# Linear attention with two MLPs: the maxima of k and q and the sums of q as rows through DRAM in blocks 2 to 8

## The chip, the cores and the metric

The kernel runs on one core of a Trainium2 chip. The metric is the device time in microseconds (us) of one execution; 1617.67 us is the median of three runs of the kernel before (1616.58, 1617.67, 1617.69). The profile was taken in an execution of its own. TensorE is called PE, VectorE DVE, ScalarE ACT, GpSimd POOL, and SyncE SP; SP issues nearly all the DMAs.

## The reference

```
q, k, v: 8 batches x 8 heads x 576 x 64, f32
q_s = exp(q - max over the 64);   q_s = q_s / (sum over the 64 + 1e-9)
k_s = exp(k - max over the 576);  k_s = k_s / (sum over the 576 + 1e-9)
kv  = k_s^T v   (64 x 64 for each batch and head);   attention = q_s kv
x = attention as 4608 tokens x 512
x = elu(x @ w_in) @ w_out                       (512 -> 2048 -> 512)
h = x @ w_in2;  P = a0 + a1 h + a2 h^2 + a3 h^3
Q = 1 + |b0| |h| + |b1| h^2;  out = (P / (Q + 1e-6)) @ w_out2
```

The weights w_out of both layers come as 64-bit floats, as does w_in; the kernel makes f32 of their bits itself.

## The kernel before

The 4608 tokens are cut into nine blocks of 512 (NB = 9, j = 0 to 8), the hidden 2048 into 16 parts of 128 (KF = 16, f). One tile (L, j, f) is one part of one block in one layer: `plan_in` multiplies the block's x (four pieces of 128 x 512) with a part of w_in into a PSUM bank (L726 to L728), an elementwise chain makes g of it (`plan_elu`, or `plan_rational` in layer 1), and `plan_out` adds g times a part of w_out into four accumulators (L768). Each f32 operand is split into a high and a low fp32r part (`copy_hi` L269, `sub_lo` L272) and each product is three matmuls, so a tile is 12 + 12 matmuls of 128 x 512. There are 2 x 9 x 16 = 288 tiles. Tiles 0 to 31 are blocks 0 and 1 of layer 0, taken in parts (CUT); block j from 2 on begins at tile 16 j, and layer 1 at tile 144.

In layer 0 the attention of the next block runs between the tiles. It goes by pairs of heads: pair n = 4 j + hp covers q of block j (512 tokens) and k and v of batch j (576 tokens) for two heads. Blocks 0 and 1 are done by `plan_pair`, blocks 2 to 8 by `plan_late`. Block 8 has no batch of its own, so k and v end with n = 31 and q with n = 35.

For q, tokens lie on the partitions: `q_max` (DVE), `q_sub` (POOL), `q_exp` (ACT), `q_sum` and `q_rec` (DVE), `q_mul` (POOL), then four transposes on PE (`q_T`, L504) and a copy out of PSUM (`q_copy`, ACT, L509), which gives qT with heads and features on the partitions. For k, `k_max` (L438, DVE) takes the maximum of the five tokens that lie on a partition, a transpose on PE (`k_maxT`, L442) and a small `k_top` (L446, DVE) finish it over the partitions, and a second transpose (`k_row`, L450) of the broadcast column gives the row in PSUM that `k_sub` (L453, DVE) subtracts; `k_exp` (ACT) follows, and `kv_mm` (L464, PE) multiplies with v, with a column of ones that gives the sum. `kv_norm` and `kv_div` make kvd. `plan_x` multiplies qT and kvd for two pairs (`x_mm`, L545) and splits the result into the x of layer 0.

`plan_unit(n)` puts into one PE operation: the four transposes of q for n, `k_maxT` of n + 2, `k_row` of n + 1, and `kv_mm` of n. The program is written out by `Plan`: a list scheduler in the program that holds a cost for each operation, starts at each turn the one that can start earliest (then by due time), and writes each engine's instructions in that order. What really waits is decided on the chip by the data and the buffers. A step number r is a tile: `in_ops[tiles[r]]` as a condition means that the plan lets the operation start only when that tile's input matmuls are done, and `at_step(n)` gives the step of pair n: 21, 23.5, 26, 28.5 for block 2, and 4 n - 17 from n = 12 on. The limits on buffers (`kind`) are two for kt, two for qt, one for x. SP issues its DMAs in the order of the plan, and each waits in the queue until its data or its buffer is there.

Of the kernel before, what the change touches and what calls it, by code (L numbers as in the profile page):

```python
# [30 lines left out]
class Plan:  # L31
# [81 lines left out]
    def run(self):  # L113
# [48 lines left out]
def linear_attention_elu_rational(  # L162
# [183 lines left out]
    def plan_w2(f, which, rank, after):  # L346

        b = {}

# [4 lines left out]

        def high():
            return b["st"][:, :, 1].bitcast(F32)

# [6 lines left out]
        b["op"] = op(SP, load, after, rank, take=["st"], dma=1.3)  # L364
# [37 lines left out]
    def pair_fns(n):  # L402
# [6 lines left out]
        kkind, vkind, qkind = (("kt", "x") if j > 1 else "kt", "vb", "qt") if not first else (  # L409
# [26 lines left out]
        def k_max(e):
            km = b["km"] = at.tile([P, 2 * D], F32, tag="km", name="km", bufs=2)
            nc.vector.tensor_reduce(out=km, in_=b["kt"].rearrange("p j n -> p n j"), op=ALU.max, axis=AX.X)  # L438

        def k_maxT(e, ps=None):  # L440
            b["mt"] = (bank() if ps is None else ps)[:, 0:P]
            nc.tensor.transpose(b["mt"], b["km"], ident)  # L442
# [64 lines left out]
        def q_copy(e):  # L507
# [3 lines left out]
        b.update({f.__name__: f for f in (load_k, load_v, load_q, k_max, k_maxT, k_top, k_row, k_sub, k_exp, kv_mm, kv_norm,  # L511
                                          kv_div, q_max, q_sub, q_exp, q_sum, q_rec, q_mul, q_T, q_copy)})
        return b

    def plan_q(n, r, gate, ahead):
# [3 lines left out]
        b["q_op"] = lq = chain("load_q", (SP, b["load_q"], [gate and in_ops[tiles[int(r) - 2]]], r - 3), take=[qkind], dma=0.66)  # L519
        o = chain("q_max", (DVE(0.67), b["q_max"], [lq, gate], r))  # L520
# [4 lines left out]
        return chain("q_mul", (either, b["q_mul"], [o], r + 1.2), extra=ahead)  # L525
# [38 lines left out]
    def plan_pair(j, hp, r):  # L564
# [4 lines left out]
        o = plan_q(n, r, None, 0.0)  # L569
# [46 lines left out]
    def at_step(n):  # L616
        return max(4.0 * n - 17, 2.5 * n + 1)

    def plan_k(n):

        b = pair_fns(n)
        r = at_step(n - 2)
        b["k_op"] = l = chain("load_k", (SP, b["load_k"], [in_ops[tiles[int(r) - 3]]], r - 3), take=[b["kinds"][0]], dma=0.83)
        b["km_op"] = chain("k_max", (DVE(1.3), b["k_max"], [l, in_ops[tiles[int(r) - 1]]], r - 1), take=["km"], extra=AHEAD)

    def plan_unit(n, q_ready=None):

        r = at_step(n)
        first_k, last_k = 2 * NP, B * NP
        has = [first_k <= m < last_k for m in (n + 2, n + 1, n)]  # L630
        b = [pair_fns(m) if ok else None for m, ok in zip((n + 2, n + 1, n), has)]
        mine = pair_fns(n)
        if has[2]:
            lv = chain("load_v", (SP, mine["load_v"], [in_ops[tiles[int(r) - 3]]], r - 2), take=["vb"], dma=0.83)

        def unit(e):
            if q_ready:
                mine["q_T"](e)
            ps = bank() if any(has) else None
            if has[0]:  # L640
                b[0]["k_maxT"](e, ps)
            if has[1]:
                b[1]["k_row"](e, ps)
            if has[2]:
                b[2]["kv_mm"](e, ps)

        need, free, take = [in_ops[tiles[int(r)]]], [], ["bank"] if any(has) else []
        if has[0]:
            need.append(b[0]["km_op"])
            free.append(("km", b[0]["km_op"]))  # L650
        if has[1]:
            need.append(b[1]["top_op"])
            free.append(("top", b[1]["top_op"]))
        if has[2]:
            need += [b[2]["exp_op"], lv]
            free += [(b[2]["kinds"][0], b[2]["k_op"]), ("vb", lv)]
            take.append("kvd")
        if q_ready:
            need.append(q_ready)
            free.append(("qt", mine["q_op"]))  # L660
            take += ["bank", "qT"]
        u = chain("unit", (PE(0.15 + 0.1 * has[0] + 0.1 * has[1] + 0.65 * has[2] + 0.4 * bool(q_ready)), unit, need, r + 1),
                  take=take, free=free, extra=0.2)
        done = []
        if has[0]:
            b[0]["top_op"] = o = chain("k_top", (DVE(0.3), b[0]["k_top"], [u], r + 1.1), take=["top"], extra=AHEAD)
            done.append(o)
        if q_ready:
            mine["t_op"] = u
            mine["qc"] = chain("q_copy", (ACT(), mine["q_copy"], [u], r + 1.1), extra=AHEAD)  # L670
        if has[1]:
            o = chain("k_sub", (DVE(0.85), b[1]["k_sub"], [u], r + 1.2))
            done.append(o)
            b[1]["exp_op"] = chain("k_exp", (ACT(0.75), b[1]["k_exp"], [o], r + 1.3), extra=AHEAD)
        if has[2]:
            o = chain("kv_norm", (DVE(0.33), mine["kv_norm"], [u], r + 1.15))
            kv_ready[n] = o = chain("kv_div", ((("ACT", 0.31), ("DVE", 0.25)), mine["kv_div"], [o], r + 1.2), extra=AHEAD)
            kvd_of[n] = u
            done.append(o)
        if done:  # L680
            at_ops.append(op((("", 0.0),), lambda e: None, done, r, free=[("bank", u)]))
        if q_ready:
            at_ops.append(op((("", 0.0),), lambda e: None, [mine["qc"]], r, free=[("bank", u)]))

    def plan_late(j, hp):
        n = j * NP + hp
        if n == 2 * NP:
            for m in (n, n + 1):
                plan_k(m)
                plan_unit(m - 2)  # L690
        if n + 2 < B * NP:
            plan_k(n + 2)
        r = at_step(n)
        plan_unit(n, plan_q(n, r - 1, in_ops[tiles[int(r) - 1]], AHEAD))
        if hp % 2:
            plan_x(n, r, [state[n - 1]["qc"], state[n]["qc"]])
# [355 lines left out]
def _laid_out(name, a, np):  # L1052
# [3 lines left out]
    if name == "q":  # L1056
        b, h, s, d = a.shape
        a = a.transpose(0, 2, 1, 3).reshape(b * s // TB, P, 4, h // 2, 2 * d).transpose(0, 3, 1, 2, 4)
        a = a.reshape(b * s // TB, h // 2, P, 4 * 2 * d)
# [42 lines left out]
```

## Time and profile before

| what | value |
|---|---|
| runs | 1616.58, 1617.67, 1617.69 us |
| profiled execution | 1616.44 us |
| its span in the profile | 1614.7 us |
| PE, ACT, DVE, POOL busy | 98%, 63%, 61%, 48% of the span |
| mean granted clock of PE | 0.995 |
| bytes moved by DMA | 114.82 MB, 71 GB/s over the span |

A row of the page names a line of the kernel, an engine, an operation, and out<-in by the program's names. Busy time is the union of a group's instructions; the duration of one matmul is longer than its distance to the next, because they are pipelined. A wait is idle time of an engine, put down to the instruction that ended it.

### The profile page before, as it was taken

The numbers are of one execution on the slowest core, as the hardware profiler recorded it, in microseconds if no ns is written. First come the engines' busy times: TensorE is split into PE (matmuls) and PEld (weight loads), VectorE is DVE, ScalarE is ACT, GpSimd is POOL, SyncE is SP. The second block draws the span as 40 slices with busy tenths as digits, with TensorE's granted clock in tenths as the row PEclk, the third lists the DMA queues.
The fourth block names the chain that finished last, engine by engine and source line by source line (L and its number), as shares of the span: only waits on it lengthen the run. The fifth ranks groups of instructions, "written<-read, shape, count | busy, mean of one in ns | idle before, by whom it ended". The sixth has DMA issues, their size and how long they took to land.

```text
span 1614.7 us, 21797 instructions
## 1 busy us (share of the span) xinstructions
PE 1584.6 (98%) x8040; PEld 1364.2 (84%) x8040; DVE 979.9 (61%) x1390; ACT 1018.6 (63%) x1688; POOL 772.0 (48%) x562
## 2 busy tenths in 40 slices
PE   6999999999999999999999999999999999999998
PEld 4788888888888888888888888888888888888886
DVE  7897655445344444321125777776868677777676
ACT  6766544454454544443557777777777777777675
POOL 3334333333233322333566666666566666666554
PEclk9999999999999999999999999999999999999999
DMA  8522533232233222110433010101000010100000
GB/s 322 203 118 89 166 120 103 100 114 86 102 102 115 85 92 81 61 40 14 124 93 103 8 53 1 52 1 39 15 26 28 20 34 10 43 8 21 1 27 26
DMA packets 48778, 114.82 MB, mean 71 GB/s; under 512 B 5664, under 2 KB 5664, under 8 KB 46624
## 3 DMA queue, kind: packets, MB, share of 16 engines
q1 hardware_dynamic: 48096, 112.10, 20.1%
q8 instruction: 63, 1.03, 0.3%
q10 hardware_dynamic: 576, 1.33, 0.2%
q14 instruction: 43, 0.35, 0.1%
HBM read 84.05 MB, written 29.36 MB: 70 GB/s over the span
## 4 chain that ended last, share of the span: by engine, by line
PE 87%; issue 4%; ACT 4%; DVE 2%; POOL 2%; DMA 1%; POOLq 0%; SPq 0%; DVEq 0%; ACTq 0%
PE acc L768 42%; PE ps L726 14%; PE ps L728 14%; PE ps L727 14%; POOL gs L272 2%; PE ps L464 1%; PE ps L545 1%; PE ps L504 1%; ACT p L871 1%; ACT s L867 1%; ACT m L877 0%; DMA hc<-w 0%; DMA kt<-in_k_dram 0%; ACT m L880 0%; PE acc L464 0%
## 5 line engine op out<-in xcount | busy, mean ns | idle before, releaser
L726 PE MATMUL ps<-xs,w_in 128*128 128x512 f32 x1152 | 438.8, 381 | 1.8 <-DVE p L892 1.7
L727 PE MATMUL ps<-xs,w_in 128*128 128x512 f32 x1152 | 436.6, 379 | 0.0
L728 PE MATMUL ps<-xs,w_in 128*128 128x512 f32 x1152 | 436.6, 379 | 0.0
L768 PE MATMUL acc<-gs,w_out 128*128 128x512 f32 x1728 | 407.1, 383 | 5.9 <-POOL gs L272 3.2
L272 POOL TENSOR_TENSOR gs<-m,gs 128x512 fp32r<-128x512 f32 x130 | 177.9, 1369 | 413.4 <-ACT gs L269 413.4
L768 PEld LDWEIGHTS acc<-gs,w_out 128*128 128x128 f32 x1728 | 324.9, 190 | 58.3 <-POOL gs L272 4.7
L838 DVE SCALAR_TENSOR_TENSOR m<-m,ps 128x512 f32<-128x512 f32 x144 | 98.9, 687 | 291.8 <-ACT m L835 278.9
L726 PEld LDWEIGHTS ps<-xs,w_in 128*128 128x128 f32 x1152 | 217.7, 189 | 37.2 <-issue 5.3
L728 PEld LDWEIGHTS ps<-xs,w_in 128*128 128x128 f32 x1152 | 217.7, 189 | 30.8
L727 PEld LDWEIGHTS ps<-xs,w_in 128*128 128x128 f32 x1152 | 217.7, 189 | 30.5
L874 POOL TENSOR_TENSOR s<-s,m 128x512 f32<-128x512 f32 x144 | 219.4, 1524 | 12.6 <-ACT m L863 12.6
L272 POOL TENSOR_TENSOR gs<-p,gs 128x512 fp32r<-128x512 f32 x72 | 116.1, 1613 | 211.7 <-issue 172.8
L768 PE MATMUL acc<-w_out,gs 128*128 128x512 f32 x864 | 200.9, 382 | 2.8 <-ACT gs L269 1.6
L768 PE MATMUL acc<-w_out,g 128*128 128x512 f32 x864 | 199.8, 379 | 0.5 <-POOL g L272 0.5
L832 ACT ACTIVATE m<-ps 128x512 f32<-128x512 f32 x144 | 85.8, 596 | 178.3 <-PE ps L728 122.5
L768 PEld LDWEIGHTS acc<-w_out,gs 128*128 128x128 f32 x864 | 164.3, 190 | 27.5 <-ACT gs L269 2.0
L768 PEld LDWEIGHTS acc<-w_out,g 128*128 128x128 f32 x864 | 163.2, 189 | 24.0 <-POOL g L272 0.9
L892 DVE SCALAR_TENSOR_TENSOR p<-p,a_sb,ps 128x512 f32<-128x512 f32 x144 | 107.5, 747 | 91.2 <-ACT m L863 91.1
L871 ACT ACTIVATE p<-ps,a_sb 128x512 f32<-128x512 f32 x144 | 112.2, 779 | 79.1 <-POOL gs L272 73.4
L269 ACT ACTIVATE gs<-m 128x512 fp32r<-128x512 f32 x144 | 90.4, 628 | 112.5 <-PE acc L768 97.7
L883 DVE SCALAR_TENSOR_TENSOR s<-s,m 128x512 f32<-128x512 f32 x144 | 135.4, 940 | 24.1 <-ACT m L880 23.9
L896 DVE SCALAR_TENSOR_TENSOR p<-p,a_sb,m 128x512 f32<-128x512 f32 x144 | 142.0, 986 | 2.3
(102 smaller groups left out, 1817.5 us busy)
## 6 DMA issues: line engine op xcount, KB each, us to landing
kt<-in_k_dram SPq DMA_DIRECT2D x32, 320.0 KB, 3.1
x<-e SPq DMA_DIRECT2D x36, 256.0 KB, 2.0
e<-x SPq DMA_DIRECT2D x36, 256.0 KB, 3.1
out_dram<-e SPq DMA_DIRECT2D x36, 256.0 KB, 2.0
vb<-in_v_dram SPq DMA_DIRECT2D x28, 325.0 KB, 3.4
bits<-in_moe_w_in_dram SPq DMA_DIRECT2D x8, 1024.0 KB, 10.3
qt<-in_q_dram SPq DMA_DIRECT2D x32, 256.0 KB, 3.2
bits<-in_moe_w_out_dram SPq DMA_DIRECT2D x8, 1024.0 KB, 11.9
```

The source lines that it names most:

```text
L269: nc.scalar.activation(out=hi, in_=src, func=AF.Copy)
L272: engine[e].tensor_tensor(out=lo, in0=src, in1=hi.bitcast(F32), op=ALU.subtract)
L726: nc.tensor.matmul(o, w[:, 0, kk, :], two(x[:, 0]), start=(kk == 0), stop=False)
L727: nc.tensor.matmul(o, w[:, 0, kk, :], two(x[:, 1]), start=False, stop=False)
L728: nc.tensor.matmul(o, w[:, 1, kk, :], two(x[:, 0]), start=False, stop=(kk == KD - 1))
L768: nc.tensor.matmul(turned(o), lhsT, two(rhs), start=(f == f0 and n == 0), stop=(f == f1 and n == 2))
L838: nc.vector.scalar_tensor_tensor(out=b["m"], in0=b["m"], scalar=-1.0, in1=b["h"], op0=ALU.add, op1=ALU.max)
L871: nc.scalar.activation(out=b["p"], in_=b["h"], func=AF.Identity, scale=a_sb[:, 3:4], bias=a_sb[:, 2:3])
L874: engine[e].tensor_tensor(out=b["s"], in0=b["s"], in1=b["a"], op=ALU.add)
L883: nc.vector.scalar_tensor_tensor(out=b["s"], in0=b["s"], scalar=1.0 + 1e-6, in1=b["a"], op0=ALU.add, op1=ALU.mult)
L892: nc.vector.scalar_tensor_tensor(out=b["p"], in0=b["p"], scalar=a_sb[:, 1:2], in1=b["h"], op0=ALU.add, op1=ALU.mult)
L896: nc.vector.scalar_tensor_tensor(out=b["p"], in0=b["p"], scalar=a_sb[:, 0:1], in1=b["a"], op0=ALU.add, op1=ALU.mult)
```

## The change

For blocks 2 to 8 the host passes two layouts of k and of q: as before, and transposed. The maximum of k is one DVE reduction over the 576 columns of transposed k (`k_top`, negated). Its 128 values are stored to DRAM one by one (`put_top`) and loaded back as a row broadcast to 128 partitions (`get_row`); `k_sub` adds this row from SBUF. The maxima and reciprocal sums of q are computed as before from q with tokens on the partitions, stored to DRAM (`put_q`) and loaded back as rows, each head's row broadcast to its 64 partitions (`get_q`). The transposed q is loaded by itself (`load_qT`), and the subtraction, the exponential and the product are done on it. `k_maxT`, `k_row`, and in these blocks `q_T`, `q_copy` and `q_mul`, go. The steps of block 2 become 18, 21, 24, 27, and k and q are begun nine tiles ahead of their step. The buffer x holds the two rows of q; it was a third buffer for k. BOUNCE and LATE are times that the plan adds to the end of these DMAs.

```diff
+    BOUNCE = 8.0
+    LATE = 4.0
...
+        def load_kT(e):
+            b["kT"] = at.tile([P, NS * 2 * D], F32, tag="kt", name="kT", bufs=2)
+            nc.sync.dma_start(out=b["kT"][:, 0:S], in_=k[1, j, hp, :, 0:S])
 
         def k_top(e):
             b["top"] = at.tile([P, 1], F32, tag="top", name="top", bufs=2)
-            nc.vector.tensor_reduce(out=b["top"], in_=b["mt"], op=ALU.max, axis=AX.X)
+            nc.vector.tensor_reduce(out=b["top"], in_=b["kT"][:, 0:S], op=ALU.max, axis=AX.X, negate=True)
+
+        def put_top(e):
+            nc.sync.dma_start(out=top_d[n].rearrange("o p -> p o"), in_=b["top"])
+
+        def get_row(e):
+            b["row"] = at.tile([P, 2 * D], F32, tag="row", name="row", bufs=2)
+            nc.sync.dma_start(out=b["row"], in_=top_d[n][0].partition_broadcast(P))
...
+        def put_q(e, key):
+            nc.sync.dma_start(out=q_d[n, key].rearrange("h (p i) -> p h i", i=4), in_=b[key].rearrange("p (h i) -> p h i", h=2))
+
+        def get_q(e, key):
+            if key == "mx":
+                b["bc"] = at.tile([P, 2, TB], F32, tag="x", name="bc", bufs=1)
+            for h in range(2):
+                nc.sync.dma_start(out=b["bc"][h * D:(h + 1) * D, int(key == "sm")], in_=q_d[n, key][h].partition_broadcast(D))
+
+        def load_qT(e):
+            b["qT"] = f32_tile("qT", 2, at)
+            nc.sync.dma_start(out=b["qT"], in_=q[1, j, hp])
+
+        def qT_sub(e):
+            engine[e].tensor_tensor(out=b["qT"], in0=b["qT"], in1=b["bc"][:, 0], op=ALU.subtract)
+
+        def qT_exp(e):
+            nc.scalar.activation(out=b["qT"], in_=b["qT"], func=AF.Exp)
+
+        def qT_mul(e):
+            engine[e].tensor_tensor(out=b["qT"], in0=b["qT"], in1=b["bc"][:, 1], op=ALU.mult)
...
     def at_step(n):
-        return max(4.0 * n - 17, 2.5 * n + 1)
+        return max(4.0 * n - 17, 3.0 * n - 6)
+
+    def gate(r):
+        return in_ops[tiles[int(r)]]
+
+    def plan_late_k(n):
 
         b = pair_fns(n)
         r = at_step(n)
+        l = chain("load_k", (SP, b["load_kT"], [gate(r - 9)], r - 9), take=["kt"], dma=0.75, extra=LATE)
+        top = chain("k_top", (DVE(0.75), b["k_top"], [l, gate(r - 8)], r - 8), take=["top"], free=[("kt", l)])
+        o = chain("put", (SP, b["put_top"], [top], r - 7.9), free=[("top", top)], extra=BOUNCE)
+        row = chain("get", (SP, b["get_row"], [o], r - 7.5), take=["row"], extra=BOUNCE)
+        l = chain("load_k", (SP, b["load_k"], [gate(r - 5)], r - 5), take=["kt"], dma=0.83, extra=LATE)
+        lv = chain("load_v", (SP, b["load_v"], [gate(r - 4)], r - 4), take=["vb"], dma=0.83, extra=LATE)
+        o = chain("k_sub", (DVE(0.85), b["k_sub"], [l, row], r - 2.5), free=[("row", row)])
+        o = chain("k_exp", (ACT(0.75), b["k_exp"], [o], r - 2.4), extra=AHEAD)
 
         def unit(e):
+            b["kv_mm"](e, bank())
+
+        u = chain("unit", (PE(0.8), unit, [o, lv, gate(r)], r + 1), take=["bank", "kvd"], free=[("kt", l), ("vb", lv)],
+                  extra=0.2)
...
+    def plan_late_q(n):
+
+        b = pair_fns(n)
+        r = at_step(n)
+        lq = chain("load_q", (SP, b["load_q"], [gate(r - 9)], r - 9), take=["qt"], dma=0.66, extra=LATE)
+        m = chain("q_max", (DVE(0.67), b["q_max"], [lq, gate(r - 8)], r - 8))
+        pm = chain("put", (SP, lambda e: b["put_q"](e, "mx"), [m], r - 7.9), extra=BOUNCE)
+        o = chain("q_sub", (POOL(), b["q_sub"], [m], r - 7.9))
+        o = chain("q_exp", (ACT(0.65), b["q_exp"], [o], r - 7.8))
+        o = chain("q_sum", (DVE(0.67), b["q_sum"], [o], r - 7.5), free=[("qt", lq)])
+        o = chain("q_rec", (DVE(0.38), b["q_rec"], [o], r - 7.4))
+        gm = chain("get", (SP, lambda e: b["get_q"](e, "mx"), [pm], r - 6.5), take=["x"], extra=BOUNCE)
+        pr = chain("put", (SP, lambda e: b["put_q"](e, "sm"), [o], r - 6.4), extra=BOUNCE)
+        b["t_op"] = lt = chain("load_qT", (SP, b["load_qT"], [gate(r - 5)], r - 5), take=["qT"], dma=0.66, extra=LATE)
+        gr = chain("get", (SP, lambda e: b["get_q"](e, "sm"), [pr], r - 5.5), extra=BOUNCE)
+        o = chain("qT_sub", (POOL(), b["qT_sub"], [lt, gm], r - 3))
+        o = chain("qT_exp", (ACT(0.65), b["qT_exp"], [o], r - 2.9))
+        b["qc"] = chain("qT_mul", (POOL(), b["qT_mul"], [o, gr], r - 2), free=[("x", gm)], extra=AHEAD)
```

## Rows read from the trace of the kernel before

**Rows 1.** Page part 1: engine, busy us, share of the span, instructions

```profile
PE 1584.6 (98%) x8040; PEld 1364.2 (84%) x8040; DVE 979.9 (61%) x1390; ACT 1018.6 (63%) x1688; POOL 772.0 (48%) x562
```

**Rows 2.** Page part 2: 40 slices, tenths busy; PEclk: granted clock

```profile
PE   6999999999999999999999999999999999999998
...
PEclk9999999999999999999999999999999999999999
```

**Rows 3.** Busy time by window: span, each engine (instructions), PEclk, DMA share, GB/s

```profile
80.00:160.00 80.00, 77.55 (x360) 67.28 (x359) 68.02 (x64) 54.58 (x72) 30.72 (x17) 1.00 0.28 108
...
200.00:660.00 460.00, 460.00 (x2609) 394.53 (x2608) 216.14 (x381) 226.69 (x388) 144.59 (x118) 1.00 0.30 101
660.00:770.00 110.00, 110.00 (x552) 93.65 (x551) 26.35 (x47) 45.51 (x78) 31.27 (x27) 1.00 0.09 29
```

**Rows 4.** Waits of PE over the whole span: us in total, times, longest us

```profile
PE acc L768 <- POOL gs L272: 4.4, 5, 1.4
...
PE ps L442 <- DVE m L838: 1.0, 1, 1.0
```

**Rows 5.** Timeline of PE around one unit: start, us, engine, line, operation

```profile
501.24 0.38 PE L728 MATMUL ps<-xs,w_in 128*128 128x512 f32 x1
501.46 0.60 PE L504 MATMUL ps<-ident,qt 128*128 128x128 f32 x4
501.89 0.27 PE L442 MATMUL ps<-ident,km 128*128 128x128 f32 x1
502.00 0.27 PE L450 MATMUL ps<-ident,top 128*128 128x128 f32 x1
502.20 0.80 PE L464 MATMUL ps<-vb,kt 128*64 128x65 f32 x20
```

**Rows 6.** Timeline of PE where L545 follows a 128x512 matmul

```profile
483.83 0.38 PE L728 MATMUL ps<-xs,w_in 128*128 128x512 f32 x1
484.14 1.09 PE L545 MATMUL ps<-qT,kvd 64*64 64x320 f32 x16
```

**Rows 7.** Groups by line, PE: count, busy us, mean ns, idle before

```profile
L504 PE MATMUL ps<-ident,qt 128*128 128x128 f32 x128 | 19.3, 273 | 0.0
...
L442 PE MATMUL ps<-ident,km 128*128 128x128 f32 x24 | 6.6, 275 | 1.0 <-DVE m L838 1.0
```

**Rows 8.** Groups by line, the other engines

```profile
L438 DVE TENSOR_REDUCE km<-kt 128x128 f32<-128x640 f32 x24 | 30.8, 1283 | 6.4 <-DMA kt<-in_k_dram 6.3
...
L453 DVE TENSOR_TENSOR kt<-kt,ps 128x640 f32<-128x640 f32 x24 | 19.3, 803 | 0.0
...
L446 DVE TENSOR_REDUCE top<-ps 128x1 f32<-128x128 f32 x24 | 6.9, 289 | 22.6 <-PE ps L464 22.5
...
L575 DVE TENSOR_REDUCE top<-kt 128x1 f32<-128x576 f32 x8 | 5.9, 734 | 0.9 <-DMA kt<-in_k_dram 0.9
...
L272 DVE TENSOR_TENSOR gs<-m,gs 128x512 fp32r<-128x512 f32 x14 | 13.0, 928 | 32.8 <-ACT gs L269 32.8
...
L498 POOL TENSOR_TENSOR qt<-qt,sm 128x512 f32<-128x512 f32 x32 | 38.3, 1196 | 47.5 <-DVE sm L495 43.6 <-ACT kvd L474 3.4 <-ACT m L832 0.5
...
L487 ACT ACTIVATE qt<-qt 128x512 f32<-128x512 f32 x32 | 19.9, 623 | 18.8 <-POOL qt L483 18.6
...
L509 ACT ACTIVATE qT<-ps 128x512 f32<-128x512 f32 x36 | 21.0, 583 | 4.5 <-PE ps L504 4.5
```

**Rows 9.** DMA issues: out<-in, queue, count, KB each, median us to landing

```profile
kt<-in_k_dram SPq DMA_DIRECT2D x32, 320.0 KB, 3.1
...
b_sb<-in_moe_b_dram SPq DMA_DIRECT2D x1, 1.0 KB, 5.8
```

**Rows 10.** Timeline of SP: one issue of a load

```profile
449.44 0.42 SPq L433 DMA_DIRECT2D qt<-in_q_dram  x1
```

**Rows 11.** Timeline of POOL in the early stretch

```profile
80.37 1.29 POOL L272 TENSOR_TENSOR gs<-m,gs 128x512 fp32r<-128x512 f32 x1 [1.23 <-ACT gs L269]
...
116.44 3.91 POOL L272 TENSOR_TENSOR gs<-m,gs 128x512 fp32r<-128x512 f32 x1 [3.54 <-ACT gs L269]
```

More of the change, by code (lines that the diff above doesn't have):

```diff
@@ L212, in linear_attention_elu_rational @@
     x1_d = {(j, i): dram.tile([P, TB], F32, name=f"x1_{j}_{i}") for j in range(NB) for i in range(KD)}
+    top_d = {n: dram.tile([1, P], F32, name=f"top_{n}") for n in range(2 * NP, B * NP)}
+    q_d = {(n, i): dram.tile([2, TB], F32, name=f"q_{i}_{n}") for n in range(2 * NP, NB * NP) for i in ("mx", "sm")}
     a_sb = main.tile([P, 4], F32, name="a_sb")
@@ L362, in save @@
             nc.sync.dma_start(out=w2_d[f, which], in_=front())
-        b["op"] = op(SP, load, after, rank, take=["st"], dma=1.3)
+        b["op"] = op(SP, load, after, rank, take=["st"], dma=1.3, extra=2.0)
         o, x = plan_f32(b["op"], lambda: b["st"], high, DM, rank, [], front)
@@ L432, in load_q @@
             qt = f32_tile(*(("e", 4) if first else ("qt", 2, at)))
-            nc.sync.dma_start(out=qt, in_=q[j, hp])
+            nc.sync.dma_start(out=qt, in_=q[0, j, hp])
             b["qt"] = qt.rearrange("p (n d) -> p n d", d=D)
[L436 to L442, printed above, removed]
+        def load_kT(e):
+            b["kT"] = at.tile([P, NS * 2 * D], F32, tag="kt", name="kT", bufs=2)
+            nc.sync.dma_start(out=b["kT"][:, 0:S], in_=k[1, j, hp, :, 0:S])
@@ L509, in q_copy, with plan_q @@
             nc.scalar.activation(out=b["qT"], in_=b["pt"], func=AF.Copy)
-        b.update({f.__name__: f for f in (load_k, load_v, load_q, k_max, k_maxT, k_top, k_row, k_sub, k_exp, kv_mm, kv_norm,
-                                          kv_div, q_max, q_sub, q_exp, q_sum, q_rec, q_mul, q_T, q_copy)})
+        b.update({f.__name__: f for f in (load_k, load_v, load_q, load_kT, k_top, put_top, get_row, k_sub, k_exp, kv_mm,
+                                          kv_norm, kv_div, q_max, q_sub, q_exp, q_sum, q_rec, q_mul, q_T, q_copy,
+                                          put_q, get_q, load_qT, qT_sub, qT_exp, qT_mul)})
         return b
-    def plan_q(n, r, gate, ahead):
+    def plan_q(n, r):
         b = pair_fns(n)
@@ L518, in plan_q @@
         either = EITHER if n < NP else POOL()
-        b["q_op"] = lq = chain("load_q", (SP, b["load_q"], [gate and in_ops[tiles[int(r) - 2]]], r - 3), take=[qkind], dma=0.66)
-        o = chain("q_max", (DVE(0.67), b["q_max"], [lq, gate], r))
+        b["q_op"] = lq = chain("load_q", (SP, b["load_q"], (), r - 3), take=[qkind], dma=0.66)
+        o = chain("q_max", (DVE(0.67), b["q_max"], [lq], r))
         o = chain("q_sub", (either, b["q_sub"], [o], r))
@@ L524, in plan_q @@
         o = chain("q_rec", (DVE(0.38), b["q_rec"], [o], r + 1))
-        return chain("q_mul", (either, b["q_mul"], [o], r + 1.2), extra=ahead)
+        return chain("q_mul", (either, b["q_mul"], [o], r + 1.2))
     def plan_x(n, r, qc):
@@ L626, in plan_unit @@
-    def plan_unit(n, q_ready=None):
         r = at_step(n)
[L629 to L634, printed above, removed]
-        def unit(e):
[L637 to L683, printed above, removed]
@@ L685, in plan_late @@
     def plan_late(j, hp):
         n = j * NP + hp
[L687 to L694, printed above, removed]
+        if n < B * NP:
+            plan_late_k(n)
+        plan_late_q(n)
         if hp % 2:
-            plan_x(n, r, [state[n - 1]["qc"], state[n]["qc"]])
+            plan_x(n, at_step(n), [state[n - 1]["qc"], state[n]["qc"]])
```

36 lines of the change are left out of this document (18 added, 18 removed).

## Prediction

> **What bounds the kernel.** I read the engines' shares first, then the slices, the windows and PE's waits. PE is busy 98% of the span, the next engine 63% [rows 1]; by slices PE is at 9 tenths or more from the second to the last but one, and the granted clock is at 9 tenths or more everywhere [rows 2]; from 80 us on it is 1.00, the level of 2.4 GHz [rows 3]. Between 200 and 660 us PE is busy for all of 460 us, while DVE has 216 us of work, ACT 227, POOL 145 and the DMA engines a 0.30 share [rows 3]. Over the whole span PE's named waits outside the start are POOL's 4.4 us in five pieces and a few of 1 or 2 us, one of them 1.0 us in front of a transpose of L442 [rows 4]. So a microsecond of PE work taken out is a microsecond of span, and work added to the other engines, SP or DMA costs only where it makes PE wait. Busy time does not price a PE instruction, since starts overlap; I price by the distance from one start to the next.
>
> **What is removed on PE.** A whole unit (22 of them, n = 8 to 29) holds pair n's four turns of q, the first turn of k for n + 2, the second for n + 1, and pair n's kv_mm; the others hold fewer. In a whole one the four transposes of L504 start at 501.46, L442 at 501.89, L450 at 502.00, and the products of L464 at 502.20 [rows 5]. That is 0.43 us for the four, 0.11 for L442, and 0.20 for L450. Of this last 0.20, 0.09 is no transpose: PE changes from 128 x 128 to 128 x 64 weights there. The same change behind an ordinary matmul costs the same: L545's narrow products start 0.31 behind L728's start, where the next 128x512 matmul would start 0.22 behind (as L504 does behind L728 [rows 5]), so 0.09 again [rows 6]. It stays, in front of kv_mm. Removed are thus 28 times the four transposes (n = 8 to 35), 28 x 0.43 = 12.0 us, and 48 single ones (24 of L442, 24 of L450), 48 x 0.11 = 5.3 us: **17.3 us**. Bounds: 19.5 if the 0.09 goes with them in the 24 units that have kv_mm (17.3 + 24 x 0.09), 15.1 if kv_mm alone has to pay it a second time. The kv_mm products, the x_mm products and all 128x512 matmuls stay.
>
> The groups give 273 and 275 ns as the mean of one transpose [rows 7]. The Trainium skill (TensorE: Matmul & The Clock Gate, Part 4: PE-mode transpose) has about 275 ns for a transpose in a kernel's context; the trace agrees on that length. By it as a price the sum would be 160 x 0.275, 44 us; by the starts in rows 5 it is 17.3, and I keep the starts, as the four of L504 lie 0.43 us long, not 1.1.
>
> **What changes on the other engines.** DVE: k_max over 640 elements, 1.28 us, and the small k_top, 0.29, go; a k_top over 576 elements comes, which blocks 0 and 1 do in 0.73 [rows 8]. That is 24 x (1.28 + 0.29 - 0.73) = 20 us less. k_sub now has both operands in SBUF: from 0.80 with the row in PSUM, up to 1.16 by the ELU subtraction whose operands both lie in SBUF (0.93 for 512 elements, times 640/512) [rows 8], 24 x 0.36 = 8.6 us at most. ACT: the copy out of PSUM, 0.58, gives place to a second exponential, 0.62 [rows 8]: 28 x 0.04 = 1.1 us. POOL: q_mul turns into qT_mul, and qT_sub is new, some 1.2 to 1.4 us each by q_mul and the POOL subtractions (1.20 and 1.29) [rows 8, 11]: 28 x 1.4 = 39 us more. All of it is priced at nothing: over 200 to 660 us the idle time is 244 us on DVE, 233 on ACT and 315 on POOL [rows 3]. Were the cover gone, the POOL part alone would cost 39 us.
>
> **DMA and SP.** A unit with k issues 13 DMAs in place of 3: the transposed k (295 KB), the row's store and its broadcast load, k, v, q, two stores of 4 KB, four broadcast loads of 128 KB, and the transposed q (262 KB). Ten more issues at 0.42 us [rows 10] are 4 us of SP in the about 21 us of four tiles. The bytes added are 24 x (295 + 66 KB) + 28 x (262 + 524 KB), 31 MB in about 560 us, 55 GB/s beside 101 at a share of 0.30 [rows 3]: share about 0.46, not full. The trip of a row through DRAM is two hops. No row shows a store of 4-byte pieces. From below a hop is bounded by 0, since it can lie wholly beside other work, and as a duration the nearest row is b_sb, 1 KB spread over the partitions, 5.8 us, and k's load of 320 KB, 3.1 us [rows 9]. I take 5.8 for each, as the pieces are small: load 3.1, k_top 0.7, two hops 11.6, together 15.4 us. The time that it has: two kt buffers serve three live tiles, so the transposed k of n + 2 gets its buffer when unit n is done, near step r + 1, and its k_sub stands at r + 8 - 2.5 = r + 5.5. That is 4.5 tiles of 24 matmuls at 0.22, 24 us. It is in time by 8 us, and its cost is nothing. What queues behind a late row is DVE's ELU step (L838) at the head of its own queue, and the stores of SP.
>
> **The early stretch.** With at_step(8) = 18 where it was 21, and q and k begun nine tiles ahead, the maxima of n = 8 go to tile 10 and those of n = 9, 10, 11 to tiles 13, 16 and 19. They fall into 80 to 160 us, where DVE has 68 of 80 us of work, preparing layer 0's weights [rows 3]. Eight POOL operations (four q_sub, two qT_sub, two qT_mul) fall there too, about 10 us onto 31 [rows 3], and there a POOL subtraction that takes 1.29 us alone took up to 3.91 [rows 11]. With 17 POOL operations in the window PE is idle for 2.4 us [rows 3]; eight more by that proportion give 1.2. From below it is -1.0: the wait in front of L442 goes with L442 [rows 4]. From above it is each of the eight costing PE the mean POOL wait, 4.4 / 5 = 0.9, 7 us. I take 1, by the window's own row.
>
> **Sum.** The profiled execution took 1616.4 us (span 1614.7 and 1.7 around it); 1616.4 - 17.3 + 1 = 1600.1. The median of the runs, 1617.67, lies 1.2 above it, so in the measure of the runs 1601.3; I say **1601**. Its own range is 1596 (the 19.5, the wait gone, and a little of the other short waits) to 1605 (15.1, and 3 us of new waits).
>
> **Rivals.** *Early contention:* DVE and POOL hold each other up, PE waits for the ELU's last step at most of the eight added POOL operations: 7 us, with a longer piece or two 10. Time 1608. For it: the 3.91. Against it: PE is short of only 2.4 us in that whole window [rows 3]. Chance 0.16, with 1605 to 1614.
>
> *Gain given back:* x_mm of a block ends later because qT or kv comes a little late, and the next block's first tile waits: seven blocks at 2.0 to 2.9 us, (17.3 - 3.2) / 7 to (17.3 + 3.2) / 7, give all of it back. Time 1617. For it: x_mm's place two tiles behind r is unchanged, so nothing has been won there. Against it: kv's unit keeps its place too, and PE shows no such wait now. Chance 0.05.
>
> *Rows come late, slower than before:* k_sub parks at the head of DVE's queue, the ELU behind it. Lateness is 3.8 + 2 hops - 24; the ELU has some 4 us to spare: its products are planned 2.5 tiles behind the start of a tile's first matmul, 1.5 or 8 us behind the last, and its own steps take 4 (three on ACT near 0.6, one on DVE near 0.9, one on POOL of 1.3 [rows 8, 11]). So it decides from a hop of 12 us on. At 13 us a hop PE loses 1.8 us in each of 24 units, 43 us: 1601 + 43 = 1644. For it: 5.8 us is one transfer at a share above half, and the store is in smaller pieces than any row shows. Against it: it needs twice the slowest small transfer. Chance 0.08. The Trainium skill (DMA: Bandwidth & Descriptors, Anatomy of one DMA) gives about 2.0 us of fixed cost; by it two hops are 4 us and this rival could not come; no run here shows a 4-byte store.
>
> *Transposes cost their length:* 160 x 0.273 = 44 us [rows 7], 1574. Against it stand the starts of rows 5. The page named above speaks for it. Chance 0.03.
>
> **Chances.** The forecast 0.68, contention 0.16, given back 0.05, late rows 0.08, full length 0.03. What lies within 0.2% of 1617.67 (1614.4 to 1620.9), about what this kernel's runs can tell from no change, is the third: same 0.05. Faster are the forecast, contention and full length, 0.87; slower 0.08. A range of 1596 to 1613 holds the forecast and nearly all of the contention, some 0.8.
>
> **What would show it.** Right: L504 only in blocks 0 and 1 (16 + 16 instances), no L442 or L450, PE still at 40 of 40 us in every window of 200 to 660 us, and a 128x512 matmul directly in front of kv_mm. The broadcast loads should land within 6 us. Contention would show as waits of L768 for L272 between 80 and 180 us; late rows as DVE waiting for a DMA in front of k_sub, and PE behind it; given back as PE idle in front of L545 or of a block's first tile. The prediction is wrong if PE's waits behind 80 us grow by over 10 us, or if a unit's kv_mm is stretched by waits for its weights.

## The result, and the profile after

The changed kernel took 1633.95 us (median of five runs), the kernel before 1617.69 in the same measurement: a ratio of 1.0093, interval 1.0068 to 1.0118. One of the five, 2057.06 us at a mean granted clock of 0.753, fell in a slow state and is not in the ratio; the other four took 1629.68 to 1637.54. Forecast were 1601 us and a range of 1596 to 1613; the kernel is slower by 0.9%, not faster. The profiled execution took 1629.7 us, 13.3 us more than the one before.

The page of the changed kernel: engines, then the granted clock and the DMA engines' busy share in 40 slices, in tenths.

```profile
PE 1580.9 (97%) x7880; PEld 1351.7 (83%) x7880; DVE 978.1 (60%) x1383; ACT 1013.1 (62%) x1680; POOL 802.1 (49%) x581
...
PEclk8999999999999999999999999999999999999999
DMA  7565986665756667321333000000001010100000
```

PE is busy 3.7 us less than in [rows 1], yet the span is longer. The DMA row, in the slices of the attention, stands at 5 to 9 tenths. The windows of [rows 3] after the change:

```profile
80.00:160.00 80.00, 76.31 (x367) 65.65 (x366) 70.63 (x76) 55.65 (x77) 37.49 (x23) 1.00 0.57 144
...
200.00:660.00 460.00, 444.90 (x2420) 373.02 (x2419) 211.16 (x371) 217.66 (x374) 159.74 (x128) 0.98 0.67 150
```

Between 200 and 660 us PE was full [rows 3]; now it is busy for 444.9 of 460 us, its mean clock is 0.98, and the DMA share is 0.67 where it was 0.30. The waits of PE from 60 to 800 us (us in total, times, longest), first before (the other wait of this stretch is the 1.0 of L442 in [rows 4]), then after:

```profile
PE acc L768 <- POOL gs L272: 2.1, 2, 1.4
```

```profile
PE acc L767 <- ACT gs L274: 8.6, 6, 2.2
PE acc L767 <- POOL gs L277: 8.5, 10, 1.4
PE ps L725 <- DVE m L837: 2.2, 1, 2.2
```

The part of the change that takes work off PE does what it says: PE has 160 matmuls fewer (7880, 8040 before), the 112 and 48 transposes of the prediction. This is the unit on PE now, to be held against [rows 5]: kv_mm starts 0.31 us behind L727's start, so the 0.09 for the change of weights is there.

```profile
234.33 0.38 PE L727 MATMUL ps<-xs,w_in 128*128 128x512 f32 x1
234.64 0.80 PE L488 MATMUL ps<-vb,kt 128*64 128x65 f32 x20
```

The other engines' groups (count | busy, mean ns | idle before) and the landings of the DMAs (KB each, median us), for [rows 8] and [rows 9]:

```profile
L455 DVE TENSOR_TENSOR kt<-kt,row 128x640 f32<-128x640 f32 x24 | 21.7, 905 | 0.0
...
L445 DVE TENSOR_REDUCE top<-kT 128x1 f32<-128x576 f32 x24 | 17.9, 745 | 13.1 <-DMA kT<-in_k_dram 13.0
...
L475 ACT ACTIVATE qT<-qT 128x512 f32<-128x512 f32 x28 | 17.4, 620 | 9.1 <-POOL qT L472 9.1
...
L472 POOL TENSOR_TENSOR qT<-qT,bc 128x512 f32<-128x512 f32 x28 | 38.1, 1360 | 2.3 <-DMA qT<-in_q_dram 2.3
```

```profile
st<-in_moe_w_in_dram SPq DMA_DIRECT2D x16, 512.0 KB, 5.2
w<-st SPq DMA_DIRECT2D x32, 256.0 KB, 4.7
...
bc<-q_mx SPq DMA_DIRECT2D x56, 128.0 KB, 5.8
...
row<-top SPq DMA_DIRECT2D x24, 64.0 KB, 5.7
...
q_mx<-mx SPq DMA_DIRECT2D x28, 4.0 KB, 8.0
...
top<-top SPq DMA_DIRECT2D x24, 0.5 KB, 8.2
```

k_top takes 0.75 us, k_sub 0.91, the second exponential 0.62, qT_sub 1.36. The small stores, which carry 0.5 and 4 KB, take some 8 us to land, longer than the other loads and stores shown here, which carry up to 512 KB; and the store of a layer 1 weight (w<-st), which landed in 2.0 us, takes 4.7.

**Where PE loses the time.** The stall at 210 us, followed back. The L-numbers of the changed kernel are: L367 the store of a prepared layer 1 weight, L357 the load of the next one into the same buffer st, L298 and L306 the first steps on it on DVE and ACT, L498 `kv_div`, L274 and L277 the high and low part of g, L767 the products that need g. First SP, then DVE, ACT and PE (start, us; the idle time before and its releaser in brackets):

```profile
196.72 0.33 SPq L367 DMA_DIRECT2D w<-st  x1
...
201.54 0.33 SPq L357 DMA_DIRECT2D st<-in_moe_w_out_dram  x1
```

```profile
206.20 0.75 DVE L298 TENSOR_SCALAR st<-st 128x512 int16<-128x512 int16 x1 [3.67 <-DMA st<-in_moe_w_out_dram]
```

```profile
206.99 0.94 ACT L306 ACTIVATE st<-st 128x512 f32<-128x512 f32 x1 [2.30 <-DVE st L298]
209.34 0.31 ACT L498 ACTIVATE kvd<-ps,rs 128x64 f32<-128x64 f32 x1 [1.42 <-DVE rs L494]
209.56 0.62 ACT L274 ACTIVATE gs<-m 128x512 fp32r<-128x512 f32 x1
```

```profile
210.23 0.48 PE L767 MATMUL acc<-gs,w_out 128*128 128x512 f32 x1 [1.92 <-ACT gs L274]
211.64 0.79 PE L767 MATMUL acc<-gs,w_out 128*128 128x512 f32 x1 [0.93 <-POOL gs L277]
```

The store goes out at 196.72. The next weight's load may not overwrite st before it has landed, and is issued at 201.54, 4.8 us later. DVE stands idle for 3.67 us at the head of its queue until the weight lands. ACT waits 2.30 us for DVE's step on the weight and then 1.42 us for a small step of DVE (L494) that stands behind it in DVE's queue; only then comes L274, the high part of g. PE waits 1.92 and then 0.93 us. There are six such pairs of waits, near 211, 228, 263, 336, 541 and 613 us. Behind five of them the clock falls, not behind the one at 228 (0.82 and 0.86 us). The view by windows (the number behind the engines is the granted clock):

```profile
205.00:210.00 5.00, 3.31 (x16) 2.56 (x14) 2.88 (x8) 1.59 (x3) 0.00 (x0) 1.00 0.99 51
210.00:215.00 5.00, 3.85 (x10) 2.93 (x11) 0.69 (x1) 2.41 (x5) 2.54 (x2) 0.66 0.69 169
...
263.00:268.00 5.00, 4.55 (x11) 3.65 (x12) 1.47 (x3) 2.23 (x4) 1.66 (x2) 0.50 0.61 172
```

At 263 to 268 us it is 0.50, the level of 1.2 GHz, after PE had waited 2.16 and 0.93 us; at 210 to 215 it is 0.66 as a mean. By windows of 40 us, the ones in which it fell:

```profile
200.00:240.00 40.00, 35.47 (x196) 28.55 (x195) 15.92 (x42) 18.75 (x35) 14.32 (x13) 0.96 0.86 182
240.00:280.00 40.00, 36.92 (x183) 30.43 (x182) 20.95 (x36) 16.81 (x29) 13.39 (x11) 0.91 0.69 140
320.00:360.00 40.00, 37.81 (x198) 31.81 (x197) 15.71 (x29) 16.13 (x29) 9.70 (x8) 0.96 0.75 167
520.00:560.00 40.00, 38.05 (x194) 31.61 (x193) 20.70 (x31) 19.63 (x35) 13.76 (x12) 0.96 0.64 140
600.00:640.00 40.00, 37.73 (x197) 31.70 (x197) 17.58 (x30) 16.19 (x29) 9.72 (x8) 0.96 0.69 177
```

**The books.** 4 x 0.04 x 40 + 0.09 x 40 = 10.0 us of PE at full speed are lost to the clock. The waits between 60 and 800 us grew from 3.1 to 19.3 us (8.6, 8.5 and 2.2 above), 16.2 more. With 17.3 us of transposes gone this makes +8.9; behind 800 us PE waits 0.9 us more (5.9 in all where it was 5.0). The measured difference is +13.3, so some 3.5 us are not named by a row. They do not lie in the waits: PE's idle time over the span grew by 16.9 us (30.1 to 47.0), which the named waits cover, so the rest is in its busy time, which fell by 3.7 us and not by 17.3 - 10.0 = 7.3.

### The profile page after: what moved, and what is told of

Read it like the earlier page. It is cut to its first block, busy times and chain, and to the rows that moved or that the text cites. A ratio compares the mean times of both kernels' runs of the same rounds, so it can differ in the third digit from the quotient of the medians.

```text
span 1627.9 us, 21893 instructions
## 1 busy us (share of the span) xinstructions
PE 1580.9 (97%) x7880; PEld 1351.7 (83%) x7880; DVE 978.1 (60%) x1383; ACT 1013.1 (62%) x1680; POOL 802.1 (49%) x581
## 4 chain that ended last, share of the span: by engine, by line
PE 73%; DMA 11%; ACT 5%; DVE 4%; issue 4%; POOL 2%; SPq 1%; POOLq 0%; DVEq 0%; ACTq 0%
PE acc L767 36%; PE ps L725 12%; PE ps L727 11%; PE ps L726 11%; DMA w<-st 3%; DMA st<-in_moe_w_in_dram 2%; POOL gs L277 2%; DMA st<-in_moe_w_out_dram 1%; PE ps L570 1%; PE ps L488 1%; DMA e<-part 1%; DMA qt<-in_q_dram 1%; DMA top<-top 1%; ACT p L870 1%; DMA bits<-in_moe_w_out_dram 1%
## 5 line engine op out<-in xcount | busy, mean ns | idle before, releaser
L727 PE MATMUL ps<-xs,w_in 128*128 128x512 f32 x1152 | 438.0, 380 | 0.0
L767 PE MATMUL acc<-gs,w_out 128*128 128x512 f32 x1728 | 416.9, 388 | 20.3 <-POOL gs L277 9.7
L767 PEld LDWEIGHTS acc<-gs,w_out 128*128 128x128 f32 x1728 | 327.5, 192 | 79.2 <-ACT gs L274 14.6
L277 POOL TENSOR_TENSOR gs<-m,gs 128x512 fp32r<-128x512 f32 x121 | 164.0, 1356 | 372.7 <-ACT gs L274 361.3
L727 PEld LDWEIGHTS ps<-xs,w_in 128*128 128x128 f32 x1152 | 218.7, 190 | 31.2
L277 POOL TENSOR_TENSOR gs<-p,gs 128x512 fp32r<-128x512 f32 x72 | 116.1, 1612 | 210.0 <-issue 172.5
L767 PE MATMUL acc<-w_out,gs 128*128 128x512 f32 x864 | 200.8, 382 | 2.7 <-ACT gs L274 1.6
L767 PE MATMUL acc<-w_out,g 128*128 128x512 f32 x864 | 199.8, 379 | 0.5 <-POOL g L277 0.5
L767 PEld LDWEIGHTS acc<-w_out,gs 128*128 128x128 f32 x864 | 164.1, 190 | 27.5 <-POOL gs L277 2.1
L767 PEld LDWEIGHTS acc<-w_out,g 128*128 128x128 f32 x864 | 163.2, 189 | 24.0 <-POOL g L277 0.9
L274 ACT ACTIVATE gs<-m 128x512 fp32r<-128x512 f32 x144 | 90.3, 627 | 114.3 <-PE acc L767 95.5
```

Source lines behind the costliest of these rows:

```text
L274: nc.scalar.activation(out=hi, in_=src, func=AF.Copy)
L277: engine[e].tensor_tensor(out=lo, in0=src, in1=hi.bitcast(F32), op=ALU.subtract)
L727: nc.tensor.matmul(o, w[:, 1, kk, :], two(x[:, 0]), start=False, stop=(kk == KD - 1))
L767: nc.tensor.matmul(turned(o), lhsT, two(rhs), start=(f == f0 and n == 0), stop=(f == f1 and n == 2))
```

## The experiments

Each was timed against the kernel before on the same chip: e1 to e4 together on one chip, e5 to e8 on another, e9 to e11 on a third, so across these groups the ratios are compared. The edits are cut down to the lines that matter. **Theory 1:** the stores' small pieces fill the DMA engines, the weights of layer 1 pass late through their one buffer, and DVE and ACT stand at the head of their queues for them. **Theory 2:** SP stands at the head of its queue for rows that are not there, and issues the weights late. **Theory 3:** the larger loads are what fills the DMA engines.

**e1, no stores.**

```diff
-nc.sync.dma_start(out=top_d[n].rearrange("o p -> p o"), in_=b["top"])
+pass                        # put_q in the same way
-in_=top_d[n][0].partition_broadcast(P)
+in_=k[1, j, hp, 0, 0:P].partition_broadcast(P)
-in_=q_d[n, key][h].partition_broadcast(D)
+in_=q[1, j, hp, 0].partition_broadcast(D)
```

> The changed kernel without its stores of maxima and reciprocal sums (left out: the rows are loaded from rows of the inputs of the same size, so the values are wrong). Plan and order of every other instruction as in the changed kernel. Theory 1, the many 4-byte and 16-byte pieces of the stores fill the DMA engines, so that the loads of layer 1's weights (st) land late and ACT and DVE stand behind them: DMA share between 200 and 660 us from 0.67 to about 0.50, landing of st from 5.0 to under 4 us, PE's waits for L274 and L277 in that stretch from 15 us to under 4, time about 1605. Theory 2, SP stands at the head of its queue behind rows that are not there yet and issues the weight loads late: the waits of rows are gone here too, time about 1605, but the share stays near 0.60. Theory 3, the larger loads (second k and q, broadcast rows) are the load: share 0.60 or more, time 1625 to 1634.

1601.30 us, ratio 0.9901 (0.9886 to 0.9916). The window of 200 to 660 us (the last three numbers are clock, DMA share and GB/s), and the landing of a weight's store:

```profile
200.00:660.00 460.00, 460.00 (x2576) 390.71 (x2575) 223.98 (x388) 230.91 (x392) 171.06 (x136) 1.00 0.49 155
```

```profile
w<-st SPq DMA_DIRECT2D x32, 256.0 KB, 2.1
```

PE is full again and the share is 0.49; theory 3 falls, since all larger loads are still there and move 155 GB/s. Theories 1 and 2 both allow the time; the share is the one of theory 1. One expectation missed: the weights' loads (st) land in 4.5 and 5.0 us, hardly sooner than the 5.2 and 5.0 with the stores there, and not under 4. What lands sooner is the store in front of them in the one buffer, in 2.1 us where it took 4.7.

**e2, stores that nothing waits for.** Only the rows come from the inputs; the stores stay.

```diff
-in_=top_d[n][0].partition_broadcast(P)
+in_=k[1, j, hp, 0, 0:P].partition_broadcast(P)     # get_q in the same way
```

> The changed kernel with its stores, but the rows are loaded from the inputs and so wait for no store (left out: the stored values are not used). Theory 1: as the changed kernel, share 0.67, time 1626 to 1634. Theory 2: SP no longer waits for a store to land, so the weight loads go out earlier: about 1605 to 1612. Theory 3: as the changed kernel.

1630.44 us, ratio 1.0082 (1.0065 to 1.0098):

```profile
200.00:660.00 460.00, 444.86 (x2426) 373.61 (x2426) 209.96 (x371) 216.79 (x372) 159.77 (x127) 0.98 0.67 149
```

The loss is back whole, though no row waits for a store. Theory 2 falls: it is the stores' traffic, not the trip of the rows.

**e3, more time in the plan for the weights.**

```diff
-b["op"] = op(SP, load, after, rank, take=["st"], dma=1.3, extra=2.0)
+b["op"] = op(SP, load, after, rank, take=["st"], dma=1.3, extra=4.0)
-... op(SP, save, [o], rank, free=[("st", b["op"])], dma=1.0)
+... op(SP, save, [o], rank, free=[("st", b["op"])], dma=1.0, extra=3.0)
```

> The changed kernel with two numbers of the plan changed: the load of a layer 1 weight is taken to end 2 us later and its store 3 us later, so that the plan puts the steps on this weight further back in the queues of DVE and ACT. All DMAs stay. If the loss is made by DVE and ACT standing at the head of their queues for a weight that lands late (theories 1 and 3): PE's waits between 200 and 660 us fall from 15 us to under 6, time 1603 to 1615, with the DMA share still 0.6 or more. If late rows or something else than the weights hold the queues (theory 2): 1625 to 1634.

1603.05 us, ratio 0.9912 (0.9896 to 0.9929). The whole computation with all its stores. (The 2.0 came with the change; the kernel before adds nothing to this load.) The window, then DVE's waits for the weights between 160 and 700 us in the changed kernel and in this one:

```profile
200.00:660.00 460.00, 460.00 (x2576) 390.65 (x2575) 230.97 (x387) 230.33 (x391) 164.90 (x131) 1.00 0.69 151
```

```profile
DVE st L298 <- DMA st<-in_moe_w_in_dram: 56.5, 12, 9.3
...
DVE st L298 <- DMA st<-in_moe_w_out_dram: 17.4, 8, 4.3
```

```profile
DVE st L298 <- DMA st<-in_moe_w_in_dram: 7.7, 6, 3.5
...
DVE st L298 <- DMA st<-in_moe_w_out_dram: 4.6, 5, 1.9
```

The DMA engines are as busy as in the changed kernel, 0.69, but DVE's waits for weights go from 74 to 12 us and PE is full. So the congestion costs PE nothing in this window by itself; it costs because the plan had put the steps on a weight at a place in DVE's and ACT's queues where the weight was no longer in time.

**e8, the same plan numbers in the kernel before**, the control for e3.

```diff
-o["end"] = self.dma_at + 2.0
+o["end"] = self.dma_at + 2.0 + o["extra"]
...                          # and extra=4.0, extra=3.0 as in e3
```

> The kernel before with the two plan numbers of e3 (a layer 1 weight's load taken to end 4 us later than in this kernel, its store 3 us later). If e3's gain over the changed kernel is cover for DMAs that the change made late, nothing is gained here, where PE does not wait between 200 and 660 us: 1615 to 1620. If the longer times are better in themselves: under 1612.

1627.34 us, ratio 1.0064 (1.0049 to 1.0079): slower, which no theory had. PE now waits for k's and q's steps; the longest of these waits:

```profile
PE ps L442 <- DVE km L438: 2.0, 1, 2.0
```

Longer times in the plan are thus not better in themselves, and a change of two numbers moves other steps to other places: 10 us here. It also means that e3 alone would be weak evidence. What carries the cause are e1, e2 and the runs from e5 on, whose plan is that of the changed kernel or differs by one short step.

**e4, the stores added to the kernel before.**

```diff
+chain("put", (SP, b[0]["put_top"], [o], r + 1.2))                     # behind k_top
+chain("put", (SP, lambda e: b["put_q"](e, "mx"), [o], r + 0.1))       # behind q_max
+chain("put", (SP, lambda e: b["put_q"](e, "sm"), [o], r + 1.1))       # behind q_rec
```

> The kernel before with the stores of the changed kernel added (the column of maxima of k, the maxima and the reciprocal sums of q of each pair of blocks 2 to 8), which nothing reads. Theory 1: DMA share between 200 and 660 us from 0.30 to 0.45 or more, landing of st from 3.4 us to 4.5 or more, and some PE waits: 1618 to 1628. Theories 2 and 3: share under 0.35, time 1617 to 1619.

1620.02 us, ratio 1.0022 (1.0010 to 1.0033), share 0.39:

```profile
200.00:660.00 460.00, 457.17 (x2591) 391.02 (x2591) 211.94 (x381) 224.22 (x387) 144.00 (x117) 1.00 0.39 100
```

The stores alone fill 0.09 of the engines and make PE wait 2.8 us in the window, without the larger loads. The time is at theory 1's lower end and the share below its 0.45. (The loads of st land in 5.0 and 5.4 us; before it was 4.7 and 4.4, not the 3.4 of the expectation.) With the larger loads alone the share is 0.49 (e1); the two additions, 0.19 and 0.09, would make 0.58 of 0.30, and together they make 0.67.

**e5, the same bytes in pieces of 512 bytes.**

```diff
-out=top_d[n].rearrange("o p -> p o"), in_=b["top"]
+out=top_d[n], in_=ident[0:1]
-out=q_d[n, key].rearrange("h (p i) -> p h i", i=4), in_=b[key].rearrange("p (h i) -> p h i", h=2)
+out=q_d[n, key].rearrange("h (g c) -> (h g) c", g=4), in_=ident[0:8]
```

> As e2 (rows from the inputs, stored values unused), but each store writes the same bytes in pieces of 512 bytes (8 for the maxima or the sums of q, 1 for the maxima of k) from a constant tile (left out: the stored values are not the maxima and sums). Theory 1, the number of pieces is the cost: share between 200 and 660 us 0.50, time 1600 to 1605, as e1. If the cost lies in a store to DRAM as such (a write that must land, 80 of them): as e2, 1628 to 1632.

1602.31 us, ratio 0.9909 (0.9895 to 0.9924), share 0.49. So it is not 80 stores as such, but their pieces.

**e6 and e7, k's store alone and q's stores alone.** In e6 the edit of e1 is made for q only, in e7 for k only.

> The changed kernel with k's store and row as they are, without q's stores (left out: q's rows are loaded from the inputs). 3072 pieces of 4 bytes stay of some 18700. Theory 1, priced by the piece: share near 0.52, time 1601 to 1608. If one late row of k is what holds DVE: 1620 or more.

> The changed kernel with q's stores and rows as they are, without k's store (left out: k's row is loaded from the inputs). Some 15600 pieces stay. Theory 1, priced by the piece: share near 0.64, PE's waits 8 to 15 us between 200 and 660 us, time 1618 to 1630. If k's row is what holds DVE: under 1608.

e6: 1614.54 us, ratio 0.9977 (0.9959 to 0.9995); e7: 1603.20 us, ratio 0.9914 (0.9899 to 0.9929). The windows of e6 and e7, then the landing of k's store in e6 and of the store of q's maxima in e7:

```profile
200.00:660.00 460.00, 454.47 (x2520) 383.68 (x2519) 218.29 (x383) 225.24 (x386) 165.91 (x133) 1.00 0.66 153
```

```profile
200.00:660.00 460.00, 459.84 (x2574) 390.26 (x2574) 219.76 (x389) 230.61 (x392) 172.09 (x135) 1.00 0.50 155
```

```profile
top<-top SPq DMA_DIRECT2D x24, 0.5 KB, 8.2
```

```profile
q_mx<-mx SPq DMA_DIRECT2D x28, 4.0 KB, 3.6
```

This corrects theory 1: a price by the piece fails. Both times lie outside its ranges, e6 above 1608 and e7 below 1618; nor does e6 reach the 1620 of a late row. (e7's time is also the one expected if k's row is what holds DVE, but in e2 no row waits for a store, and the loss was whole.) The 3072 pieces of k (24 x 128) lift the share from 0.49 to 0.66, the 14,336 of q (28 x 2 x 256) to 0.50. q's store lands in 3.6 us when k's is not there, in 8.0 when it is. By the ratios against e1, k's store alone costs 12 us, q's alone 2 (the intervals overlap), both in e2 29. So some 15 us come only where both are there, and without k's store, 128 pieces of 4 bytes side by side in 512 bytes of DRAM, next to nothing of the loss is left.

**e10 and e11, what about this store.** Both keep k's store alone, as e6, but take k's row from the inputs, so that nothing waits for the store: e10 with 16 bytes a piece, e11 with 4 bytes a piece, each 64 bytes from the next (the DRAM tiles are made larger to fit).

```diff
-nc.sync.dma_start(out=top_d[n].rearrange("o p -> p o"), in_=b["top"])
+nc.sync.dma_start(out=top_d[n].rearrange("o (p c) -> (o p) c", c=4), in_=ident[:, 0:4])             # e10
+nc.sync.dma_start(out=top_d[n].rearrange("o (p c) -> (o p) c", c=16)[:, 0:1], in_=b["top"])         # e11
```

> As e6 (k's store alone, q's left out), but k's store writes 128 pieces of 16 bytes from a constant tile, and k's row comes from the inputs (left out: the stored values are not the maxima). If 4 bytes as the size of a piece is the cost: share near 0.50, time 1600 to 1605. If it is a store of 128 pieces in one run of addresses, whatever their size: share 0.60 or more, 1608 to 1617, as e6.

> As e10, but 128 pieces of 4 bytes (the real maxima), each 64 bytes from the next in DRAM, read by nothing. If the size of a piece is the cost: share 0.62 or more, time 1608 to 1617, as e6. If neighbours within the same 64 bytes hold each other up: share near 0.50, time 1600 to 1605.

e10: 1599.07 us, ratio 0.9896 (0.9881 to 0.9911), share 0.50. e11: 1602.14 us, ratio 0.9912 (0.9895 to 0.9928), share 0.49. The store's landing in e10, then in e11:

```profile
top<-ident SPq DMA_DIRECT2D x24, 2.0 KB, 3.9
```

```profile
top<-top SPq DMA_DIRECT2D x24, 0.5 KB, 1.5
```

The same number of pieces of the same 4 bytes lands in 1.5 us when they lie 64 bytes apart, and in 8.2 side by side. It is neither the number nor the size alone; it is 4-byte neighbours. Distances between 4 and 64 bytes were not tried, nor what in the chip makes it so.

**e9, the whole kernel without such a store.** DVE turns the column of 128 maxima in blocks of 32 x 32, and the store has 4 pieces of 128 bytes.

```diff
+def k_flip(e):
+    b["flip"] = at.tile([P, 32], F32, tag="flip", name="flip", bufs=2)
+    nc.vector.transpose(out=b["flip"], in_=b["top"].to_broadcast([P, 32]))
-nc.sync.dma_start(out=top_d[n].rearrange("o p -> p o"), in_=b["top"])
+nc.sync.dma_start(out=top_d[n].rearrange("o (g c) -> (o g) c", g=4), in_=b["flip"][0:P:32])
+o = chain("k_flip", (DVE(0.2), b["k_flip"], [top], r - 7.95))
```

> The whole changed kernel, nothing left out, with one step more: DVE turns the column of 128 maxima of k in blocks of 32 x 32 (one short operation per pair), so that the store of k's row has 4 pieces of 128 bytes in place of 128 of 4 bytes. The plan numbers are those of the changed kernel, with 0.2 us of DVE added. If the 4-byte store is the cause (theory 1 narrowed to k's store, after e6 and e7): DMA share between 200 and 660 us 0.50, no PE waits there beyond 2 us, time 1600 to 1605. If not: 1615 or more.

1600.83 us, ratio 0.9903 (0.9888 to 0.9918): faster than both kernels. The window, PE's waits from 60 to 800 us, the new step's group, and the engines of the page:

```profile
200.00:660.00 460.00, 460.00 (x2576) 390.85 (x2575) 226.11 (x408) 230.87 (x392) 170.46 (x135) 1.00 0.50 155
```

```profile
PE acc L772 <- POOL gs L277: 2.0, 2, 1.3
PE ps L730 <- DVE m L842: 1.1, 1, 1.1
PE acc L772 <- ACT e L812: 0.7, 1, 0.7
```

```profile
L449 DVE STREAM_TRANSPOSE flip<-top 128x32 f32<-128x32 f32 x24 | 5.2, 215 | 0.5
```

```profile
PE 1566.2 (98%) x7880; PEld 1344.5 (84%) x7880; DVE 985.3 (62%) x1407; ACT 1015.0 (64%) x1681; POOL 804.3 (50%) x580
```

PE is full for all of 460 us at a share of 0.50; its waits are 3.8 us where the kernel before has 3.1. One DVE operation of 0.22 us per pair replaces a store that cost the kernel some 31 us (ratios 1.0093 and 0.9903).

## Why the prediction was wrong, step by step

- **What bounds the kernel, and the transposes' price: right.** e9 has all of the change except the form of one store. Its profiled execution took 1600.1 us, 16.3 less than before, and the sum was 1600.1. So exact a hit is in part luck: PE's busy time fell by 18.4 us (1584.6 to 1566.2) where 17.3 was forecast, and its idle time grew by 2.0 (30.1 to 32.1) where 1 was. In e1, with the same work on PE, the busy time fell by 16.6. Both lie within the bounds of 15.1 to 19.5, so the price by starts (0.11 us) holds; by lengths (44 us) it would have been the 1574 of that rival.
- **The other engines: right.** k_sub took 0.91 us (up to 1.16 foreseen), the rest came as in the rows, and e9 shows all of it covered.
- **The bytes: right.** The forecast share of 0.46 was worked out from bytes alone; the kernels that move these bytes without 4-byte neighbours show 0.49 (e1, e5) and 0.50 (e9), at 155 GB/s where 101 + 55 was forecast. The 0.67 of the changed kernel is no matter of bytes.
- **The failed step: the store of k's row, "its cost is nothing".** The prediction priced it as a hop, a duration to be hidden (5.8 us, as b_sb's load), and asked only whether the row would be late; it said itself that no row shows a store of 4-byte pieces. The row was not late: DVE shows no wait for it in front of k_sub, although store and load took 8.2 + 5.7 = 13.9 us where 11.6 was taken. The prediction left out that a transfer also occupies the 16 DMA engines while it lasts. This store lifts their share by 0.17 (e6 against e1), 0.17 x 460 = 78 us of all 16 engines, by an estimate of some 20 stores in that stretch about 4 us each. It made the wrong thing late: the weights of layer 1, which no step of the prediction names, and whose store and next load share one buffer: the store landed in 4.7 us where it was 2.0, and DVE's waits for these weights were 74 us between 160 and 700 us, where the kernel before has 14. Alone this store costs 12 us, with q's stores beside it 29.
- **What queues behind: right in kind, wrong in its place.** For the case of a late row the prediction put the ELU behind k_sub on DVE. It stands behind a late weight step on DVE and, first of all, on ACT.
- **The clock was not in the sum at all.** Behind five pairs of waits, 2 to 3 us each, the clock fell (to 0.50 at 263 to 268 us), and that cost another 10 us. A rival's price in waits has to be raised by that; at 16.2 us of waits it was over half as much again.
- **The rivals.** "Rows come late" had the right sign, but not its mechanism: its hop of 12 us was never reached (the longest store or load of a row of k took 11.3 us). The prediction's 4 us for two hops by the Trainium skill (DMA: Bandwidth & Descriptors, Anatomy of one DMA) did not come either; the page gives its about 2.0 us for DMAs issued by GpSimd, and these are issued by SP. The early stretch cost about what the forecast took, 1.2 us of PE (77.55 [rows 3] to 76.31 between 80 and 160 us), but not by its cause: PE's wait for POOL there is as it was (1.42 us, now 1.43), and what grew is a wait for DVE, from 1.03 to 2.23 us. The 2.4 us of idle time from which the price per POOL operation was taken held that 1.03 too. "Given back" did not come in the form described, as between 200 and 660 us all of PE's waits are those of L767 for g.
- **The signs that the prediction named.** PE is not at 40 of 40 us in the windows of 200 to 660 us, and its waits behind 80 us grew by 17 us where "over 10" was to prove the prediction wrong. The broadcast loads landed within the 6 us foreseen (medians 5.8, 5.1 and 5.7), so this sign was blind to the loss.

## What to carry to other kernels

When a step is moved to DMA, ask of each new transfer how long it holds the DMA engines and whose transfer then comes late, not only whether its own reader is in time; here it was the buffer with one copy and a store before its next load that suffered first. Where a column of a tile goes to DRAM as a row, don't let each partition write one 4-byte value beside its neighbour: turn it first into pieces of 128 bytes. In a program whose order is fixed ahead, a transfer that gets slower hurts at the head of in-order queues, so the plan's times for all transfers must be reviewed, and a change of these times needs its own control.

## What the runs showed of the hardware

- A store of 128 pieces of 4 bytes side by side in DRAM lands in 8.2 us and fills the DMA engines (share 0.66 in e6, 0.49 in e1); 128 pieces of 16 bytes side by side land in 3.9 us, and 4-byte pieces 64 bytes apart in 1.5 us, both at 0.49 to 0.50.
- The Trainium skill (DMA: Bandwidth & Descriptors, Specifications) says that below 512 bytes a transfer is not at line rate and is done by read-modify-write. No run here shows the read-modify-write itself. In cost the 4-byte neighbours fit it; the rest of what is below 512 bytes hardly shows: 14,336 pieces of 16 bytes lift the share by 0.01 and the time by 2 us (e7 against e1).
- Waits of PE of 1.0 to 2.2 us with a second one of 0.9 us behind a single matmul were followed by a fall of the granted clock (0.50 at 263 to 268 us); a pair of 0.82 and 0.86 us was not, nor were single waits between 80 and 160 us, where the clock stays at 1.00: 1.03 and 1.42 us in the kernel before [rows 3], 2.23 and 1.43 in the changed one.
